# Loads of the second token half's operands: issued by GpSimd instead of SyncE, in a kernel that sums a gated long convolution and a feed-forward layer

## The chip, the cores and the metric

The kernel runs on one core of a Trainium2 chip. The metric is the device time of one execution in microseconds (us), as the median of several runs. A separate execution was recorded by the hardware profiler; every view quoted below is of that one execution. The engines are PE (TensorE: matmuls; its weight loads are shown as PEld), DVE (VectorE), ACT (ScalarE), POOL (GpSimd) and SP (SyncE, which here only issues DMAs). A name with a q behind it (SPq, ACTq) is an engine's sequencer. L477 is line 477 of the kernel.

## The reference

With S = 2048 tokens, D = 576 channels and 4608 hidden units:

```python
xn = layernorm(q)
k_shift = causal_conv(k, shift_k)              # 4 taps per channel
kv = k_shift * v
y = long_causal_conv(kv, ssm_k) + kv * ssm_D   # 2048 taps per channel, by FFT
out = q + xn * y + relu(xn @ w1) @ w2          # w1: 576x4608, w2: 4608x576
```

All in float32. (q is the kernel's x.)

## The kernel before

**The feed-forward layer.** The 2048 tokens are 16 tiles of 128, in two halves of 8. A half is two blocks of 512 tokens. The hidden units are taken 256 at a time, in 18 groups for each half, so there are 36 groups of work, numbered g from 0 to 35; from g = 3 on such a group is a "quad". g = 17 (`NQ - 1`) is the last group of the first half, and g = 18 the first of the second. The first 512 of the 576 channels go through a scheme with seven products for eight (Strassen's kind). It needs seven combinations of the transposed, normalized tokens, the *operands*: "00", "01", "11", "s1", "s2", "s3", "s4", each 128 partitions x 2 x 2 x 512 numbers of 4 bytes (1 MB). The last 64 channels are done the plain way by `rest`, with one *rest operand* `hl` for each block (256 KB). Each number is split into a high and a low part, so that a product is three matmuls (high x high, high x low, low x high). Operand and weights both have the two parts.

**One quad, in PE's order.** First product "00" with weights `wa`; then "01" with `wa`, and the rest of block 0 with `wr`; "s2" with `wb`; "s1" with `wc`; "s3" with `wb`; the rest of block 0 with `wr`; "s4" with `wd`; the rest of block 1; "11" with `wc`; the rest of block 1. Between them stand eight units of the second layer (`mm2`, matmuls into `pso`) that belong to the group before. In the trace the operands are named x and xs (the digits are left out), the products' accumulators psh, and the first layer's low parts ll.

**The weights.** `load_w1(g)` fetches a group's first-layer weights into the tile r1 (0.66 MB in three DMAs, L494 and L497), `load_w2` a piece of the second layer's (288 KB, L505); after g = 0 both are issued by GpSimd. In the profile these tiles are all called r. `load_w1(g + 2)` stands near the end of quad g in the program, once the splits that read the tile before are issued: r1 has one buffer. `split_w` (L512, L513) makes the two parts: ACT writes the high one and GpSimd subtracts for the low one. `sums` (L525) adds weights on DVE for `wb` and `wc`.

**The convolution** is a stream of small steps (`conv`), taken between the products by `tick`, so that PE has their matmuls (L762, into psf and psg) among its own. It is done as a two-stage Fourier transform, with loads of k and v from SP (L164) and stores to DRAM in between (zx, zk, zy).

**The second half's operands** are made early, within the stream (`later_operands`): normalized, transposed, combined, split, and stored in DRAM (`ops_n`, `hl_n`). An operand has one buffer on the chip. So in quad 17, as soon as the product that reads an operand of the first half for the last time is traced, `later` calls `load_operand` (L477) or `load_rest_operand` (L480) for its successor. Such a load waits for that product. Quad 18 and all that follow read the new ones. There are nine of these loads: seven of 1 MB and two of 256 KB, 7.9 MB (1.05 million bytes each for the seven).

**Order.** Instructions of one engine are issued in order, so an instruction that waits holds up what stands behind it on that engine. The order is set when the kernel is built, by a scheduler that runs a model of time (`schedule_with_timeline_sim=True`): among what the model takes to be ready, it puts the earlier in the program first. `issue_after` adds an order by hand. PE's order is fixed in this way from end to end; that of GpSimd and SP is left to the scheduler, within the data's dependences. DMAs issued by SP go out on queue q1, those of GpSimd on q0, those of ACT on q10.

Of the kernel before, what the change touches and what calls it, by code (L numbers as in the profile page):

```python
# [10 lines left out]
F32 = mybir.dt.float32  # L11
# [21 lines left out]
HB = NB // HALVES  # L33
# [66 lines left out]
def h3_ffn_kernel(ctx: ExitStack, tc, x, k, v, shift_k, ssm_k, ssm_D, w1, w2, fwd, inv, mid, out):  # L100
    nc = tc.nc
# [27 lines left out]
    ops_n = {o: dram.tile([P, 2, 2, 512], F32, name=f"ops_{o}") for o in OPERANDS}  # L129
    hl_n = dram.tile([HB, P, 512], F32, name="hl_n")  # L130
# [67 lines left out]
    def operand(o, tag=None):  # L198
        xo[o] = xp.tile([P, 2, 2, 512], F32R, tag=f"x{tag or o}", name=f"x{o}")
        return xo[o]  # L200

    def rest_operand(b):
        hl[b] = xp.tile([P, 512], F32R, tag=f"hl{b % HB}", name=f"hl{b}")
        return hl[b]
# [269 lines left out]
                yield W_FS  # L474

    def load_operand(o):
        nc.sync.dma_start(operand(o).bitcast(F32), ops_n[o])  # L477

    def load_rest_operand(b):
        nc.sync.dma_start(rest_operand(b).bitcast(F32), hl_n[b - HB])  # L480

    def at_turn(g):

# [144 lines left out]
    def quad(g, units):  # L628
# [8 lines left out]
        def later(o):  # L637
            if g == NQ - 1:
                (load_operand if isinstance(o, str) else load_rest_operand)(o)
# [664 lines left out]
```

## Time and profile before

| | |
|---|---|
| median of 3 runs | 1030.0 us (1029.59 to 1030.02) |
| the profiled execution's own time | 1038.15 us |
| its span, first to last instruction | 1036.3 us |
| mean granted TensorE clock | 0.996 |
| DMA bytes moved | 184.69 MB, mean 178 GB/s |
| the nine operand loads, issued by SP | from 447.8 to 478.7 us of the span |
| quad 17, by its first product and that of quad 18 | 446.3 to 478.5 us |

The times in the views count from the start of the span. In the first part of the page each engine has its busy time, its share of the span and its number of instructions. A row of a timeline is start, duration, engine, line, operation, output<-inputs, shapes and count, with the engine's idle time before it and what ended it in brackets. A row of the DMA view is output<-input, issuing queue, count, KB each, and the median time from issue to landing.

### The profile page before, as it was taken

What the parts mean: (1) busy time and instruction counts of PE and PEld (TensorE: products, weight loads), DVE (VectorE), ACT (ScalarE), POOL (GpSimd) and SP (SyncE); (2) the same over time, 40 slices, a digit from 0 to 9 for tenths busy, and PEclk for the clock granted to TensorE, in tenths of its full rate; (3) what the DMA queues carried; (4) which work ended last, traced back from release to release, by engine and by line L of the source; (5) the groups of instructions that cost most, each with busy time, mean ns of one, the idle gap of its engine ahead of it and who ended that gap; (6) DMA issues with size and microseconds to landing.
All of it is one profiled execution on the core that took longest, in us unless ns stands there. A gap on an engine that the chain in (4) does not pass through costs nothing.

```text
span 1036.3 us, 17434 instructions
## 1 busy us (share of the span) xinstructions
PE 1019.9 (98%) x6506; PEld 846.6 (82%) x6506; DVE 702.4 (68%) x1075; ACT 431.4 (42%) x770; POOL 463.6 (45%) x502
## 2 busy tenths in 40 slices
PE   8999999999999999989999999999999999999997
PEld 5898999998988888878878888866777777788777
DVE  6787677775565556778787889455666666556764
ACT  7244334443354444434444444544444445332120
POOL 3335444555443555544555455314424245244450
PEclk9999999999999999998999999999999999999999
DMA  7114364479445473379944433677877887757684
GB/s 175 52 49 118 114 162 126 154 216 199 115 127 172 160 245 104 126 216 322 277 139 132 129 103 115 210 221 227 242 212 226 250 256 226 221 177 230 208 259 114
DMA packets 130848, 184.69 MB, mean 178 GB/s; under 512 B 69213, under 2 KB 81631, under 8 KB 129868
## 3 DMA queue, kind: packets, MB, share of 16 engines
q1 hardware_dynamic: 76180, 123.48, 39.9%
q0 software_dynamic: 16048, 52.44, 16.9%
q10 hardware_dynamic: 38536, 7.66, 3.9%
q8 instruction: 51, 0.84, 0.3%
q14 instruction: 33, 0.27, 0.1%
HBM read 119.04 MB, written 45.61 MB: 159 GB/s over the span
## 4 chain that ended last, share of the span: by engine, by line
PE 88%; DMA 4%; DVE 3%; ACT 2%; issue 1%; POOL 1%; ACTq 1%; SPq 0%; DVEq 0%; POOLq 0%
PE pso L569 40%; PE psh L569 34%; PE psf L762 6%; PE psg L762 4%; PE psh_c L569 3%; DMA r<-in_w 2%; DMA zk<-area 1%; DMA acc<-in_x 1%; ACTq L809 0%; DVE area L1047 0%; DVE area L941 0%; DVE area L942 0%; ACT x L291 0%; DMA area<-in_k 0%; DVE sums L525 0%
## 5 line engine op out<-in xcount | busy, mean ns | idle before, releaser
L569 PE MATMUL pso<-w,hh 128*128 128x288 f32 x2304 | 467.9, 296 | 0.0
L569 PEld LDWEIGHTS pso<-w,hh 128*128 128x128 f32 x2304 | 378.1, 188 | 35.9 <-issue 14.8
L569 PE MATMUL pso<-w,ll 128*128 128x288 f32 x1152 | 339.5, 295 | 0.0
L749 DVE TENSOR_TENSOR acc<-pso,acc 128x576 f32<-128x576 f32 x243 | 183.1, 754 | 167.3 <-PE pso L569 166.9
L569 PEld LDWEIGHTS pso<-w,ll 128*128 128x128 f32 x1152 | 216.4, 188 | 0.0
L513 POOL TENSOR_TENSOR wb<-sums,wb 128x512 fp32r<-128x512 f32 x33 | 52.4, 1587 | 251.1 <-ACT wb L512 217.9
L513 POOL TENSOR_TENSOR w<-r,w 128x576 fp32r<-128x576 f32 x72 | 108.2, 1510 | 118.6 <-ACT w L512 118.6
L569 PE MATMUL psh<-xs,wb 128*128 128x512 f32 x396 | 102.7, 394 | 0.0
L569 PE MATMUL psh<-x,wa 128*128 128x512 f32 x396 | 102.5, 394 | 0.1
L569 PE MATMUL psh<-hl,wr 128*128 128x512 f32 x264 | 85.7, 406 | 3.6 <-ACT psh L686 3.1
L569 PEld LDWEIGHTS psh<-x,wa 128*128 128x128 f32 x396 | 72.4, 188 | 15.3 <-ACT psh L648 0.5
L569 PEld LDWEIGHTS psh<-xs,wb 128*128 128x128 f32 x396 | 70.6, 188 | 14.6 <-issue 3.2
L513 POOL TENSOR_TENSOR wa<-r,wa 128x512 fp32r<-128x512 f32 x36 | 56.1, 1558 | 57.2 <-ACT wa L512 57.1
L762 PE MATMUL psf<-area 64*64 64x512 f32 (+10 forms) x664 | 75.2, 489 | 1.6 <-DVE area L1047 1.0
L593 DVE SCALAR_TENSOR_TENSOR ll<-psh,hh 128x512 fp32r<-128x512 f32 x66 | 45.2, 685 | 37.6 <-ACT hh L591 37.2
L686 ACT ACTIVATE psh<-psh 128x512 f32<-128x512 f32 x33 | 19.2, 582 | 116.5 <-DVE u L684 114.6
L569 PEld LDWEIGHTS psh<-hl,wr 128*128 128x128 f32 x264 | 46.3, 189 | 23.0 <-issue 10.5
L591 ACT ACTIVATE hh<-psh 128x512 fp32r<-128x512 f32 x66 | 39.3, 596 | 50.8 <-PE psh L569 50.1
L1020 ACT ACTIVATE area<-psg 128x1024 f32<-128x1024 f32 x34 | 33.0, 1024 | 53.7 <-PE psg L762 53.7
L591 ACT ACTIVATE hh<-p 128x512 fp32r<-128x512 f32 x33 | 20.9, 632 | 81.9 <-PE pso L569 46.9
L569 PE MATMUL psh<-xs,wd 128*128 128x512 f32 x198 | 52.6, 401 | 0.0
L1047 DVE TENSOR_TENSOR area<-psf,area 128x512 f32<-128x512 f32 x72 | 44.7, 682 | 11.6 <-DMA area<-area 8.4
(134 smaller groups left out, 1487.0 us busy)
## 6 DMA issues: line engine op xcount, KB each, us to landing
r<-in_w POOLq DMA_DIRECT2D x70, 288.0 KB, 3.8
area<-area SPq DMA_DIRECT2D x144, 128.0 KB, 4.0
r<-in_w POOLq DMA_DIRECT2D x35, 512.0 KB, 4.8
zk<-area SPq DMA_DIRECT2D x64, 144.0 KB, 2.2
area<-zk SPq DMA_DIRECT2D x18, 512.0 KB, 4.5
area<-zx SPq DMA_DIRECT2D x18, 512.0 KB, 4.1
zy<-area SPq DMA_DIRECT2D x36, 256.0 KB, 4.7
area<-zy SPq DMA_DIRECT2D x32, 288.0 KB, 4.3
```

Of the source, the lines that this page charges most:

```text
L513: nc.gpsimd.tensor_tensor(w[:, 1, :n], src, w[:, 0, :n], OP.subtract)
L569: last = nc.tensor.matmul(ps, a, m, start=start and n == 0, stop=n == len(seq) - 1, skip_group_check=True)
L591: done["act"] = nc.scalar.activation(hh, ps, AF.Relu)
L593: nc.vector.scalar_tensor_tensor(ll, ps, 0.0, hh, op0=OP.max, op1=OP.subtract)
L686: nc.scalar.activation(x, y, AF.Copy, scale=-1.0)
L749: done["acc"] = nc.vector.tensor_tensor(two(acc[t]), ps[:, :, :NH], two(acc[t]), OP.add)
L762: done["pe"] = nc.tensor.matmul(ps, a, m, start=start, stop=stop, skip_group_check=True)
L1020: nc.scalar.activation(dst, src, AF.Copy)
L1047: nc.vector.tensor_tensor(filt[:, c, k, :], banks[k], filt[:, c, k, :], OP.mult)
```

## The change

The two functions that load the second half's operands issue their DMA from GpSimd. Source, destination, size and the places of the calls stay the same.

```diff
     def load_operand(o):
-        nc.sync.dma_start(operand(o).bitcast(F32), ops_n[o])
+        nc.gpsimd.dma_start(operand(o).bitcast(F32), ops_n[o])
 
     def load_rest_operand(b):
-        nc.sync.dma_start(rest_operand(b).bitcast(F32), hl_n[b - HB])
+        nc.gpsimd.dma_start(rest_operand(b).bitcast(F32), hl_n[b - HB])
```

They are called in quad 17 alone, after each product that reads the old operand for the last time:

```python
def later(o):
    if g == NQ - 1:
        (load_operand if isinstance(o, str) else load_rest_operand)(o)
```

## The prediction

> **What bounds the kernel now.** I read the page first, then the waits of PE, then the chain of waits and the busy time by stage around the nine loads that move. The page:
>
> ```profile
> span 1036.3 us, 17434 instructions
> PE 1019.9 (98%) x6506; PEld 846.6 (82%) x6506; DVE 702.4 (68%) x1075; ACT 431.4 (42%) x770; POOL 463.6 (45%) x502
> PEclk9999999999999999998999999999999999999999
> ```
>
> PE is busy for 98% of the span, so a change that adds no PE work can only touch the 16.4 us in which PE is idle, and the slices in which its clock is low. There is one such slice, the nineteenth (466 to 492 us). The waits of PE over the whole span (engine and line, what it waited for, total, times, longest):
>
> ```profile
> PE psh L569 <- ACT psh L686: 3.1, 2, 2.6
> PE psg L762 <- ACT acc L742: 2.9, 1, 2.9
> ```
>
> The single wait of 2.9 us lies where the operands are reloaded. The busy time in stretches of 5 us there (PE, PEld, DVE, ACT, POOL, then granted clock, DMA share, GB/s):
>
> ```profile
> 450.00:455.00 5.00, 5.00 (x32) 4.52 (x31) 4.93 (x7) 2.39 (x4) 4.99 (x6) 1.00 0.68 229
> 455.00:460.00 5.00, 5.00 (x33) 4.62 (x32) 2.22 (x4) 1.82 (x3) 1.47 (x2) 1.00 1.02 328
> 460.00:465.00 5.00, 2.78 (x25) 1.57 (x23) 1.06 (x3) 1.07 (x3) 0.35 (x1) 0.99 1.04 286
> 465.00:470.00 5.00, 4.36 (x22) 2.76 (x23) 4.67 (x5) 3.16 (x6) 4.61 (x5) 0.50 1.01 405
> 470.00:475.00 5.00, 5.00 (x30) 4.67 (x29) 2.27 (x4) 1.12 (x2) 0.00 (x0) 0.83 1.01 367
> 475.00:480.00 5.00, 5.00 (x29) 4.36 (x28) 5.00 (x7) 2.88 (x6) 1.86 (x2) 1.00 0.77 264
> ```
>
> PE stops for 2.9 us, and then its granted clock is 0.50 and 0.83. The low clock costs 4.36 x 0.50 = 2.2 us and 5.00 x 0.17 = 0.85 us. With the 2.86 us of the stop, **this stall is worth 5.9 us**. The DMA engines are full from 455 to 475. The chain of waits says why PE stopped (start, us, what):
>
> ```profile
> 452.37 11.48 DMA r<-in_w
> 463.93 0.07 ACT wa L512
> 464.47 0.58 ACT p L669
> 465.05 0.55 ACT acc L742
> 465.64 1.99 PE psg L762 x16
> ```
>
> r is the first-layer weight tile of quad 18. GpSimd issued its three loads from 452.37, and they landed at 463.85. ACT's split of r (L512) stood first in ACT's order, and the copy that PE needed stood behind it. From landing to PE is 465.64 - 463.85 = 1.8 us, and PE was ready at 465.64 - 2.86 = 462.8: **r must land by 461.0** for no stall. What r usually takes, and what its loads cost GpSimd, from the view of tile r:
>
> ```profile
> DMA to landing us min/median/max: 2.9/4.3/11.5
> L494 POOL DMA_DIRECT2D r<-in_w x35: 756/773/952, 16.6 to 960.4; - x35
> L505 POOL DMA_DIRECT2D r<-in_w x70: 537/559/563, 23.7 to 972.1; - x70
> ```
>
> So this landing is the longest of all. What the DMA engines did while r was under way, from the DMA view of 452.4 to 463.9:
>
> ```profile
> DMA packets 786, 3.00 MB, mean 261 GB/s; under 512 B 139, under 2 KB 139, under 8 KB 603
> q1 hardware_dynamic: 503, 2.05, 65.0%
> q0 software_dynamic: 282, 0.93, 27.2%
> xs<-ops_s SPq DMA_DIRECT2D x3, 1024.0 KB, 12.8
> x<-ops SPq DMA_DIRECT2D x1, 1024.0 KB, 11.2
> area<-in_k SPq DMA_DIRECT2D x2, 144.0 KB
> ```
>
> q0 is GpSimd's queue, with r (0.66 MB) and a second-layer weight; q1 is SP's, with the operands. 3.00 MB moved before r had landed, though r and the loads issued with it or just before (operand 01 of 1.05 MB, and k and v, 0.59 MB) make only 2.3 MB. So bytes of operands issued after r, from 457.26 on, went out ahead of the last bytes of r: **the two queues share the engines, and r loses by it**.
>
> **The change part by part.** Nine issues leave SP, and nine come to GpSimd. Bytes, tiles and what each load waits for stay. The two queues around the first loads, SP's and then GpSimd's:
>
> ```profile
> 447.83 4.93 SPq L477 DMA_DIRECT2D x<-ops  x2
> 457.26 4.84 SPq L477 DMA_DIRECT2D xs<-ops_s  x3
> ```
> ```profile
> 446.93 1.75 POOL L513 TENSOR_TENSOR wb<-sums,wb 128x512 fp32r<-128x512 f32 x1 [7.14 <-ACT wb L512]
> 449.85 1.30 POOL L513 TENSOR_TENSOR wr<-r,wr 128x256 fp32r<-128x256 f32 x1
> 451.13 1.29 POOL L513 TENSOR_TENSOR wc<-sums,wc 128x512 fp32r<-128x512 f32 x1
> 452.37 0.78 POOL L494 DMA_DIRECT2D r<-in_w  x1
> 478.14 1.83 POOL L513 TENSOR_TENSOR wb<-sums,wb 128x512 fp32r<-128x512 f32 x1 [8.53 <-ACT wb L512]
> 483.51 0.77 POOL L494 DMA_DIRECT2D r<-in_w  x1
> ```
>
> *GpSimd's time.* No load of 1 MB from GpSimd is in the trace. The rows give 0.56 us for 288 KB and 0.77 us for 512 KB; scaled by bytes, 1 MB would be 1.55 us. I take 0.56 to 0.77, since r's 0.77 us belongs to a load in four pieces per partition and an operand is one piece: nine issues, 5 to 7 us (at most 12). GpSimd is idle for over half of the stage, 8.53 us in one piece ahead of 478.14, so I cost this at nothing. The place without cover is the issue of operand 00: if it stands among the splits, wr ends later than 451.15, and PE reads wr next:
>
> ```profile
> 452.22 0.62 PE L569 MATMUL psh<-hl,wr 128*128 128x512 f32 x2
> ```
>
> The slack is 1.07 us. An issue of 0.56 to 0.77 us fits; 1.55 us would cost 0.5 us.
>
> *The added waits.* Each load waits on its new engine for the last product that reads the old operand. Operand 00's is over about 447.8, while GpSimd works on wb, so it waits for nothing. Operand 01's ends about 452.4, when r is issued anyway. For s2, s1 and s3 GpSimd waits at most from 456.8 to about 461.8. Behind it stands the split of wa of quad 18, which PE needs only from 478. Nothing to pay.
>
> *What the move frees.* On one queue, operands issued after r no longer pass it. With operand 00's issue ahead and 01's behind, r goes out at about 453.0. Ahead of it or beside it are r itself, k and v, 1.25 MB, at 261 GB/s 4.8 us: r lands at about 458, 3 us before the limit. If 01's load is issued first, 1.05 MB more, it lands at about 462 and PE stops for 0.8 us, less than the other stop of the trace (2.6 us). The stall goes in both orders: **-5.9 us**, or -5.1. SP's own loads of k and v come out from behind the operands' waits. They wait for DVE later and bound nothing: 0.
>
> *What is late next.* Quad 18 starts 5.9 us earlier, but the bytes do not go faster. Its own weight load, r of quad 19, is issued at 483.51, and on ACT it reads:
>
> ```profile
> 491.58 0.64 ACT L512 ACTIVATE wa<-r 128x512 fp32r<-128x512 f32 x1 [1.10 <-DMA r<-in_w]
> 492.12 0.58 ACT L669 ACTIVATE p<-psh 128x512 f32<-128x512 f32 x1
> 493.92 0.63 PE L569 MATMUL psh<-hl,wr 128*128 128x512 f32 x2
> ```
>
> It lands late already, but PE needs the copy of 492.12 only at 493.92: slack 493.92 - 492.70 = 1.2 us. The idle DMA time that can be filled is 0.32 x 5 us in 450 to 455 and 0.23 x 5 us in 475 to 480, 2.75 us. So r of quad 19 comes 5.9 - 2.75 - 1.2 = 1.9 us too late for PE: **+1.9 us**. The ends are 0 (operand 11, in front of r on one queue, is done by then) and 4.7 us (no idle time can be used).
>
> *Sum:* -5.9 + 1.9 = **-4.0 us** on the profiled execution, whose own time is 1038.15 us. The median of the runs shown is 1030.0 us, 8 us less: the stall may be smaller where nothing is recorded, which the rivals take up. Forecast: 1030.0 - 4.0 = **1026.0 us**, its own range 1022 to 1028.
>
> **The rivals.** *The engines are shared whoever issues* (chance 0.17): the bytes are the same, the DMA share is 1.0 from 455 to 475, and r lands as late as before because it waits for bytes and not for a queue. Time 1030. The Trainium skill has this as a rule (DMA: Bandwidth & Descriptors, "Issuing engines are not separate DMA queues"): DMAs from any issuer run on the same 16 engines and interleave, and a second issuer saves only issue time. By that rule the sum would be 0. Against it stand the 3.00 MB ahead of the end of r; the same page ("Queues, rings and completion order") has each engine take turns between queue rows, which fits them.
>
> *The stall belongs to the profiled execution* (0.10): 1038.15 - 1030.0 = 8.15 us is more than the 5.9 us. Then there is nothing to win: 1030.
>
> *r queues behind the operands* (0.18), the slower side. On one queue r cannot pass what is in front of it, and the operands' landings are 11.2 and 12.8 us long in the DMA view. If GpSimd issues 01 before r, r ends behind it at 452.4 + 11.2 + 2.9 = 466.5, 2.6 us later than now. Quad 19's r, behind operand 11 (issued after the splits, about 482), ends at 482 + 11.2 + 2.9 = 496.1, 4.6 us after the 491.5 of now, of which 1.2 us is slack: +3.4 us. Together +6.0: 1036, and up to 1039 if a second low-clock stretch follows. It decides by r's landing: after 463.9, this rival is right. Against it: r's loads stand before 01's in the program, and by 452.4 both can be issued.
>
> *More than the forecast* (0.05): the 2.6 us wait for L686 goes as well, because SP's loads are earlier. 1030.0 - 5.9 - 2.6 = 1021.5.
>
> **How the numbers follow.** The forecast has 0.50, then 0.17, 0.10, 0.18 and 0.05. About 0.2% (2.1 us) is what a measurement of this kernel can tell from no change. Faster: forecast and the last, less a little for a forecast that ends within 2.1 us: 0.53. Same: 0.17 + 0.10 and that little: 0.28. Slower: 0.19, with the bound of late wr. The range takes in the forecast, both rivals at 1030 and the lower part of the slower one: 1021.5 to 1034.
>
> **What would show it.** Right: r of quad 18 lands by 461, PE's wait for L742 is gone, no low slice in PEclk; a wait for r in quad 18 of 1 to 4 us. The first step is wrong if r still takes over 10 us; the cover is wrong if PE waits for GpSimd's wr or wb. If the profile loses its stall and the times stay, the stall belonged to the profile. The prediction fails most easily by the order that the scheduler gives GpSimd's queue, which the trace of before cannot show.

## The result, and the profile after

The change makes the kernel slower. Before: 1029.8 us (1029.03 to 1030.02, 4 runs); after: 1036.01 us (1034.62 to 1036.74, 4 runs); ratio 1.006, 95% interval 1.0043 to 1.0078. In a later session it was 1035.44 us (1033.41 to 1038.55, 6 runs) against 1029.98 us (29 runs), ratio 1.0051 (1.0031 to 1.0071). So the loss is 5.5 to 6.2 us, where a gain of 4 was forecast; 1036.0 lies above the range's end of 1034.0.

The page of the changed kernel:

```profile
span 1035.0 us, 17432 instructions
PE 1019.7 (99%) x6506; PEld 846.9 (82%) x6506; DVE 705.4 (68%) x1075; ACT 431.8 (42%) x770; POOL 463.7 (45%) x511
PEclk9999999999999999999999999999999999999999
```

and the head of its PE waits over the whole span:

```profile
PE psh L569 <- ACT psh L648: 2.5, 1, 2.5
PE psf L762 <- issue: 1.4, 1, 1.4
PE psf L762 <- DVE area L1047: 1.4, 4, 0.9
```

The wait for L742 that stood in the profile of before is gone; two new ones stand in its place. The busy time in stretches of 5 us (PE, PEld, DVE, ACT, POOL, clock, DMA share, GB/s):

```profile
460.00:465.00 5.00, 5.00 (x47) 3.35 (x46) 4.42 (x5) 3.23 (x5) 4.98 (x6) 1.00 1.00 335
465.00:470.00 5.00, 5.00 (x37) 4.83 (x36) 3.29 (x5) 1.12 (x2) 1.65 (x4) 1.00 1.03 422
470.00:475.00 5.00, 5.00 (x29) 4.40 (x28) 5.00 (x6) 2.88 (x6) 2.52 (x4) 1.00 1.03 412
475.00:480.00 5.00, 2.46 (x18) 2.22 (x17) 5.00 (x5) 0.58 (x1) 4.60 (x6) 1.00 1.01 413
480.00:485.00 5.00, 5.00 (x21) 4.35 (x21) 3.87 (x6) 1.82 (x3) 0.65 (x1) 0.66 1.05 295
```

From 460 to 475, where before stopped and ran at 0.50 and 0.83, PE is full at a clock of 1.00. The stop now comes at 475 to 480, just behind the turn from quad 17 to 18 (472.5), and the low clock, 0.66, behind it. GpSimd's row at the start of the stage and ACT's split of r of quad 18, from the timeline:

```profile
448.47 1.25 POOL L513 TENSOR_TENSOR wd<-r,wd 128x256 fp32r<-128x256 f32 x1
449.67 0.55 POOL L477 DMA_DIRECT2D x<-ops  x1
450.25 0.75 POOL L513 TENSOR_TENSOR wr<-r,wr 128x256 fp32r<-128x256 f32 x1
...
452.20 0.79 POOL L494 DMA_DIRECT2D r<-in_w  x1
...
454.02 0.57 POOL L477 DMA_DIRECT2D x<-ops  x1
```
```profile
458.65 0.64 ACT L512 ACTIVATE wa<-r 128x512 fp32r<-128x512 f32 x1 [0.66 <-DMA r<-in_w]
```

The order is the one that was assumed: operand 00 among the splits, then r, then operand 01. r was there at 458.65 (forecast: about 458, against 463.85 in the one profile of before). So this part of the forecast came out. Why is the kernel slower?

### The profile page after: what moved, and what is told of

Read it like the earlier page. It is cut to its first block, busy times and chain, and to the rows that moved or that the text cites. A ratio compares the mean times of both kernels' runs of the same rounds, so it can differ in the third digit from the quotient of the medians.

```text
span 1035.0 us, 17432 instructions
## 1 busy us (share of the span) xinstructions
PE 1019.7 (99%) x6506; PEld 846.9 (82%) x6506; DVE 705.4 (68%) x1075; ACT 431.8 (42%) x770; POOL 463.7 (45%) x511
## 4 chain that ended last, share of the span: by engine, by line
PE 91%; DVE 3%; ACT 2%; DMA 1%; issue 1%; ACTq 0%; POOL 0%; SPq 0%; DVEq 0%; POOLq 0%
PE pso L569 42%; PE psh L569 35%; PE psf L762 6%; PE psg L762 4%; PE psh_c L569 3%; PE psw L1211 1%; DMA area<-area 1%; DVE area L1047 1%; DMA r<-in_w 1%; ACTq L809 0%; DVE ll L593 0%; DVE area L946 0%; DVE area L941 0%; ACT x L291 0%; DVE sums L525 0%
## 5 line engine op out<-in xcount | busy, mean ns | idle before, releaser
L762 PE MATMUL psf<-area 64*64 64x512 f32 (+10 forms) x664 | 75.4, 489 | 3.5 <-issue 1.4
L513 POOL TENSOR_TENSOR wa<-r,wa 128x512 fp32r<-128x512 f32 x36 | 53.5, 1487 | 46.5 <-ACT wa L512 46.5
L593 DVE SCALAR_TENSOR_TENSOR ll<-psh,hh 128x512 fp32r<-128x512 f32 x66 | 45.2, 685 | 38.3 <-ACT hh L591 38.2
L686 ACT ACTIVATE psh<-psh 128x512 f32<-128x512 f32 x33 | 19.2, 582 | 112.5 <-DVE u L684 110.5
L1020 ACT ACTIVATE area<-psg 128x1024 f32<-128x1024 f32 x34 | 33.0, 1024 | 55.6 <-PE psg L762 55.6
L1047 DVE TENSOR_TENSOR area<-psf,area 128x512 f32<-128x512 f32 x72 | 44.7, 682 | 15.4 <-DMA area<-area 6.5
L569 PE MATMUL psh<-x,wc 128*128 128x512 f32 x198 | 51.7, 396 | 0.0
```

The source lines that it names most:

```text
L513: nc.gpsimd.tensor_tensor(w[:, 1, :n], src, w[:, 0, :n], OP.subtract)
L569: last = nc.tensor.matmul(ps, a, m, start=start and n == 0, stop=n == len(seq) - 1, skip_group_check=True)
L593: nc.vector.scalar_tensor_tensor(ll, ps, 0.0, hh, op0=OP.max, op1=OP.subtract)
L686: nc.scalar.activation(x, y, AF.Copy, scale=-1.0)
L762: done["pe"] = nc.tensor.matmul(ps, a, m, start=start, stop=stop, skip_group_check=True)
L1020: nc.scalar.activation(dst, src, AF.Copy)
```

## The experiments

Sixteen runs, in four groups; the runs of before beside them had medians of 1029.9, 1029.8, 1030.3 and 1030.0 us. No edit changes the output. A kernel's PE order is the same in all of them (the names of the matmuls agree one by one, but for four of 6506 in one profile), so the start of the k-th matmul of a kernel less that of before, in its second profile, tells where time is lost.

### Is the stall of the profiled execution there at all?

The kernel before, profiled again.

> The kernel of before unchanged, to see an ordinary execution of it. Theory A (the profiled execution of before, 1038.15 us, was an unusual one: its two stops of PE, 2.9 us with 3.0 us of low clock behind it in quad 17 and 2.6 us in quad 19, are absent when the kernel takes 1030): span about 1028, no wait of PE for L742, granted clock 1.0 from 465 to 475, r of quad 18 landing under 10 us. Rival C (the stops are in every execution, and recording adds the rest): the stop of 2.9 us and the low clock are there again, whatever the time.

1029.2 us. The windows where the first profile had its stall and the changed kernel its stop, and ACT's split of r of quad 18:

```profile
460.00:465.00 5.00, 5.00 (x48) 3.39 (x47) 4.78 (x6) 4.24 (x7) 4.07 (x4) 1.00 1.04 348
465.00:470.00 5.00, 5.00 (x36) 4.79 (x35) 3.96 (x7) 1.12 (x2) 0.92 (x2) 1.00 1.01 413
470.00:475.00 5.00, 5.00 (x30) 4.40 (x29) 5.00 (x7) 2.89 (x6) 2.67 (x2) 1.00 1.07 402
475.00:480.00 5.00, 5.00 (x34) 4.59 (x33) 4.96 (x7) 1.45 (x3) 4.53 (x6) 1.00 1.01 304
```
```profile
460.21 0.63 ACT L512 ACTIVATE wa<-r 128x512 fp32r<-128x512 f32 x1 [2.01 <-DMA r<-in_w]
```

There is no wait for L742 and no low clock, and r was there at 460.21, ahead of the limit of 461.0, with the operands on SyncE. The other stop of the first profile (2.6 us, for L686) is missing too. Of 85 timed runs of before, the highest took 1034.86 us; the profiled one took 1038.15. The 5.9 us were **a stop that comes in some executions**: of the eleven other profiles in which SyncE issues the early operands, one has it, with 3.2 us (the kernel with operand 11 and rest 3 on GpSimd, below). In the six profiles where GpSimd issues the early operands it is not seen; but none in six against two in twelve can be chance, so it is not shown that the move prevents it.

What the move does for r is smaller than the first profile made it look. ACT's split of r began 6.4 to 6.8 us after r's issue in those six profiles, 7.1 to 8.1 us in the ten ordinary ones with SyncE, and 11.6 and 11.9 us in the two with the stop. So about 1 us of the 5 comes from the move, and the median holds nothing of it.

### Which of the nine loads costs?

Operand 11 and the rest operand of block 3, the last two of the nine, go back to SyncE; and the reverse, those two alone on GpSimd.

```diff
-        nc.gpsimd.dma_start(operand(o).bitcast(F32), ops_n[o])
+        (nc.sync if o == "11" else nc.gpsimd).dma_start(operand(o).bitcast(F32), ops_n[o])
...
-        nc.gpsimd.dma_start(rest_operand(b).bitcast(F32), hl_n[b - HB])
+        (nc.sync if b == 3 else nc.gpsimd).dma_start(rest_operand(b).bitcast(F32), hl_n[b - HB])
```

> The changed kernel, but operand 11 and the rest operand of block 3 are loaded by SyncE as before; the seven earlier loads stay on GpSimd. Theory A (the loss is at the turn from quad 17 to 18: the issues of these two loads stand ahead of and among GpSimd's splits wb, wd, wr, wc, DVE's L946 takes 3.33 us and L593 2.44 us beside them, PE waits 2.5 us and has a low clock after): 1030 to 1031.5, both DVE instructions under 2 us, no wait of PE for L648 over 1 us. Rival B (the loss comes from 7 MB of operands on GpSimd's queue, which delays the convolution's transfers or the weights): 1034 to 1036, about as the changed kernel.

> The other part alone: only operand 11 and the rest operand of block 3 go through GpSimd, the seven earlier loads through SyncE. Theory A: 1033.5 to 1036, with the stretched DVE instructions and the wait of PE at the turn of quad 17 to 18. Rival B: 1030 to 1031, since five sixths of the bytes are back on SyncE's queue.

Seven on GpSimd and the last two on SyncE: 1030.75 us (10 runs), ratio 1.0007 (0.9997 to 1.0016), and no matmul's start differs from before by more than 0.3 us from there on (0.03 us at the end). Only the last two on GpSimd: 1033.71 us (9 runs), ratio 1.0031 (1.002 to 1.0041). So seven loads of the nine cost nothing, and two cost about 4 us. In the second kernel's profile both stops are seen, the chance one and the one of the change (PE's waits, 440 to 500):

```profile
PE psg L762 <- ACT acc L742: 3.2, 1, 3.2
PE psh L569 <- ACT psh L648: 2.6, 1, 2.6
```

### What the last two do at the turn

The timeline of the changed kernel from 472 (start, us; DVE's operations beside GpSimd's):

```profile
472.46 0.53 POOL L477 DMA_DIRECT2D x<-ops  x1 [4.60 <-PE psh L569]
...
472.70 3.33 DVE L946 TENSOR_TENSOR area<-area 128x576 f32<-128x576 f32 x1
473.01 1.30 POOL L513 TENSOR_TENSOR wb<-sums,wb 128x512 fp32r<-128x512 f32 x1
...
474.27 0.73 POOL L513 TENSOR_TENSOR wd<-r,wd 128x256 fp32r<-128x256 f32 x1
474.95 0.57 POOL L480 DMA_DIRECT2D hl<-hl_n  x1
475.54 1.08 POOL L513 TENSOR_TENSOR wr<-r,wr 128x256 fp32r<-128x256 f32 x1
475.95 2.44 DVE L593 SCALAR_TENSOR_TENSOR ll<-p,hh 128x512 fp32r<-128x512 f32 x1
...
476.59 1.26 POOL L513 TENSOR_TENSOR wc<-sums,wc 128x512 fp32r<-128x512 f32 x1
...
479.09 0.58 ACT L648 ACTIVATE psh<-psh 128x512 f32<-128x512 f32 x1 [5.31 <-DVE ll L593]
```

and of before (the second profile):

```profile
472.33 1.83 POOL L513 TENSOR_TENSOR wb<-sums,wb 128x512 fp32r<-128x512 f32 x1 [6.40 <-ACT wb L512]
...
472.91 1.85 DVE L946 TENSOR_TENSOR area<-area 128x576 f32<-128x576 f32 x1
...
474.11 1.25 POOL L513 TENSOR_TENSOR wd<-r,wd 128x256 fp32r<-128x256 f32 x1
...
474.69 1.22 DVE L593 SCALAR_TENSOR_TENSOR ll<-p,hh 128x512 fp32r<-128x512 f32 x1
...
476.60 0.58 ACT L648 ACTIVATE psh<-psh 128x512 f32<-128x512 f32 x1 [2.61 <-DVE ll L593]
```

In before GpSimd and DVE take turns: each operation waits for one of the other engine's (wd takes 1.25 us for the 0.73 it needs, L946 1.85 for 0.75). In the changed kernel the load of operand 11 waits for the product that reads the old one, until 472.46, and so stands directly ahead of the split of wb. Then wb and wd run one after the other at full speed and DVE's L946 waits for both; L593 waits for wr and wc. L648, which PE needs, comes at 479.09 and not at 476.60, 2.5 us late, and PE stops for 2.5 us.

The Trainium skill (SBUF — State Buffer, "Who interferes with whom") states that a DVE instruction with two inputs in SBUF contends with a GpSimd instruction that reads SBUF, and calls the port pair that they share an exclusive lock. The trace agrees in kind: L946 and the L593 on p and hh are held up, while in before the L593 on psh (in PSUM) takes its 0.68 us beside wr. The section does not say that DVE's waiting operation is passed by several of GpSimd's in a row, which these rows show.

Four kernels take the two issues apart. First, the two loads are left where they are on GpSimd but carry 8 bytes of each partition; SyncE loads the rest (in the line below, `some` is true for these two loads). Then each load alone:

```diff
+    def parts(to, src, some): [q.dma_start(to[:, s], src[:, s]) for q, s in (((nc.gpsimd, slice(0, 2)), (nc.sync, slice(2, None))) if some else ((nc.sync, slice(0, None)),))]
```
```diff
+        (nc.gpsimd if o == "11" else nc.sync).dma_start(operand(o).bitcast(F32), ops_n[o])
```
```diff
+        (nc.gpsimd if b == 3 else nc.sync).dma_start(rest_operand(b).bitcast(F32), hl_n[b - HB])
```

> The kernel before, but of operand 11 and of rest operand 3 GpSimd loads the first 8 bytes of each partition, at the places where the changed kernel issues them (ahead of wb, and between wd and wr), and SyncE all the rest. The bytes are as before on SyncE's queue; what comes to GpSimd is two issues and their waits. If the issues among GpSimd's splits make the loss at the turn (they hold the splits up or bring them beside DVE's operations): the additions of DVE in 472 to 479 take over 2 us as in the changed kernel, PE stops for about 2.5 us and the clock falls after it, 3 to 4 us, 1032.5 to 1034. If the bytes on GpSimd's queue make it: DVE's operations take 0.7 us, no stop, 1029 to 1030.5.

> The kernel before, with only operand 11 loaded by GpSimd (ahead of the split of wb of quad 18; 1 MB). If this issue alone brings GpSimd's splits beside DVE's additions at the turn: DVE over 2 us for one of them, a stop of PE of 2 to 3 us, 1032 to 1034 as with both. If the issue of rest operand 3, between wd and wr, does it: no loss here, 1029 to 1030.5. If it takes both, half of it or less: 1030.5 to 1031.5.

> The kernel before, with only the rest operand of block 3 loaded by GpSimd, between the splits of wd and wr of quad 18. In the trace of before the four splits there alternate with DVE's operations (L946 1.85 us, L593 1.22). If an issue directly ahead of a row of splits lets GpSimd's splits pass DVE one after another: the alternation holds until the issue, then the operation of DVE that comes up during it waits for wr and wc and takes over 2 us; the copy for PE (L648) is late by 0 to 1.5 us and the loss at the turn is 0 to 1.5 us; 1030 to 1031.5. If the issue alone costs (0.55 us of GpSimd, no passing): no operation of DVE over 2 us, no loss; 1029 to 1030.5.

With slivers of 8 bytes: 1033.92 us (5 runs), ratio 1.0038 (1.0026 to 1.0051), L946 3.34 us, L593 2.44, PE's wait for L648 2.5. So **it is the issue, not the bytes**. Operand 11 alone: 1034.90 us (5 runs), ratio 1.0041 (1.0027 to 1.0056); in its profile 2.4 us are lost at the turn, and 3.3 at a stop at 520 such as the first profile of before has too (2.3 us), so its time is not the price of the issue alone. Rest operand 3 alone: 1029.85 us (11 runs), ratio 0.9998 (0.9988 to 1.0009), no operation of DVE at the turn over 1.9 us. So it is the issue ahead of wb; the one between wd and wr costs nothing, and the half of its expectation that saw DVE passed there was wrong. With operand 11 alone, nothing stands between the four splits, and the timeline shows the plain case:

```profile
472.55 0.53 POOL L477 DMA_DIRECT2D x<-ops  x1 [7.20 <-PE psh L569]
...
472.79 4.87 DVE L946 TENSOR_TENSOR area<-area 128x576 f32<-128x576 f32 x1
473.10 1.30 POOL L513 TENSOR_TENSOR wb<-sums,wb 128x512 fp32r<-128x512 f32 x1
...
475.75 1.28 POOL L513 TENSOR_TENSOR wc<-sums,wc 128x512 fp32r<-128x512 f32 x1
```

L946 began before wb and ended at 477.66, 0.6 us after wc. In the changed kernel DVE got through at the issue of rest 3, between wd and wr, but PE's stop is no shorter for it (2.5 us, against 2.3 with operand 11 alone). The trace of before shows the same once, where it costs PE nothing, at the end of quad 21:

```profile
585.31 0.54 POOL L815 DMA_DIRECT2D area<-in_fwd  x1 [6.24 <-PE psf L762]
585.51 3.65 DVE L942 TENSOR_TENSOR area<-area 128x576 f32<-128x576 f32 x1
...
585.86 1.29 POOL L513 TENSOR_TENSOR wb<-sums,wb 128x512 fp32r<-128x512 f32 x1
```

The fourth kernel keeps all nine on GpSimd but issues the last two behind the splits:

```diff
+    def late_loads():
+        with tc.issue_after(done["pool"].ins): load_operand("11"), load_rest_operand(3)
...
-            if g == NQ - 1:
+            if g == NQ - 1 and o not in ("11", 3):
...
-        split_c(g)
+        split_c(g); g == NQ and late_loads()
```

> All nine loads stay on GpSimd; operand 11 and the rest operand of block 3 are issued behind the split of wc of quad 18, and not ahead of wb and between wd and wr. Theory A: 1030 to 1031.5, since GpSimd's splits start as early as before, with nothing between them; it tells the place of the two issues from the engine that makes them. Rival B: 1034 to 1036.

1034.06 us (6 runs), ratio 1.0042 (1.0027 to 1.0057). The time is the one that was expected of the rival, and the trace shows why it does not speak for it. The turn is free: DVE and GpSimd alternate as in before, and PE does not stop. But 1.1 us are lost at 493 (r of quad 19 is issued behind operand 11 and comes late), and 2.0 us at 677 to 684. ACT's row of the first:

```profile
490.81 0.63 ACT L512 ACTIVATE wa<-r 128x512 fp32r<-128x512 f32 x1 [1.72 <-DMA r<-in_w]
```

### The second loss, 200 us later

The changed kernel also loses 2.1 us at 677 to 684 (before's time; 1.7 us in its second profile), in quad 25, long after the loads. The load concerned is that of r of quad 26; the expectations name it by the quad in which it is issued, 25, and the next one likewise. The chain in the second profile of the changed kernel (1033.88 us):

```profile
665.09 0.77 POOL L494 DMA_DIRECT2D r<-in_w  x1 [1.12 <-issue]
...
669.34 0.63 ACT L512 ACTIVATE wa<-r 128x512 fp32r<-128x512 f32 x1 [0.55 <-DMA r<-in_w]
669.88 2.04 ACT L1020 ACTIVATE area<-psf 128x512 f32<-128x512 f32 x4
...
671.45 2.52 SPq L1025 DMA_DIRECT2D area<-area  x4
...
678.88 2.49 DVE L1047 TENSOR_TENSOR area<-psf,area 128x512 f32<-128x512 f32 x4 [5.29 <-DMA area<-area]
680.27 1.07 PE L762 MATMUL psf<-area 64*64 64x512 f32 x4 [1.03 <-issue]
```

The issue of r begins 1.12 us after GpSimd is done with the split before it, and no row says what it waits for. r is late, ACT's split of it stands in front of the copies L1020, the copies' stores L1025 go out late, and PE waits for what DVE makes of them. Less the 2.0 us by which this kernel is late already, the split begins 0.6 us later than in before and L1047 1.7 us later; how the one grows to the other is not shown. In the three kernels run until then that have this wait (the changed one, the last two loads alone on GpSimd, and those two behind the splits; in the second it stands one load of r later, at 705), the DMAs that GpSimd had issued until then come to **28,416 rows** (a row is one piece of a transfer, as the trace's record of the issue counts them: 512 + 64 + 64 for the three loads of r, 128 for a second-layer load, 128 for an operand). The theory: GpSimd waits when its count of rows passes a fixed place, and nine loads more, 1152 rows, bring that place from a harmless issue to the one of r. Nine small DMAs in quad 20 add the rows without the operands, and nine of 16 rows the number without the rows:

```diff
+    nc.gpsimd.memset(sign, 1.0); pad = const.tile([P, 18], F32, name="pad")
...
+    def extra():
+        with tc.issue_after(done["pool"].ins): [nc.gpsimd.dma_start(pad[:128, 2 * i:2 * i + 2], w1[:128, 2 * i:2 * i + 2]) for i in range(9)]
...
-        split_w2(g, 1)
+        split_w2(g, 1); g == 20 and extra()
```

> The kernel before, with all nine operand loads on SyncE, and nine more DMAs from GpSimd in quad 20, each 128 rows of 8 bytes into a tile that nobody reads. So GpSimd has issued as many DMAs and as many rows as in the changed kernel by quad 23, while neither operands nor traffic move. Theory D (GpSimd stops before an issue when its count of DMA rows reaches a fixed place, 28,416 rows in the three kernels that show it): the L494 of r of quad 25 waits 1.1 us at about 662, r lands later, and PE loses 1.4 to 2 us at 670 to 680, none at the turn from quad 17 to 18; time 1031 to 1032. Theory L (the count of DMAs and not of rows shifts which semaphores they use): the same. Theory O (the late r belongs to the operands' loads themselves): no wait there, 1029 to 1030.

> As the kernel with nine extra DMAs of 128 rows, with 16 rows each: nine DMAs more, but 144 rows in place of 1152. Theory D: the place of 28,416 rows is reached about 1,000 rows later than there, at the issue of another load, so the L494 of r of quad 25 waits for nothing and PE loses nothing at 670 to 680; 1029 to 1030. Theory L: the wait of 1.1 us stays at the same L494, and the time is that of the kernel with 128 rows.

> The kernel with nine extra DMAs of 128 rows once more, for a second profile: its profiled execution was the fastest of five (1032.4, median 1035.1). If the rest of the loss lies at the late r of quad 25 too: PE loses 3 to 6 us at 670 to 690, against 2.6 us in the first profile. If the nine issues cost by themselves: a loss in quads 20 and 21, at 560 to 590.

> The kernel with nine extra DMAs of 16 rows once more, for a second profile: its median was 2.7 us above before, and the first profile shows no loss at quads 20 to 26. If the nine issues cost by themselves: a loss at 560 to 590 here. If the shifted place costs, now at the L494 of r of quad 26: a loss at 700 to 725. If neither: 1029 to 1031, and chance.

128 rows: the wait of 1.12 us at that load is there, at 28,416 rows, and PE loses 2.4 us at 677 in the first profile and 3.2 in the second. 16 rows: no wait there and 0.3 us lost at 677; the wait has moved one quad on, to a place where r has time:

```profile
697.92 0.77 POOL L494 DMA_DIRECT2D r<-in_w  x1 [1.23 <-issue]
```

There 28,304 rows had been issued, and this load's 512 end at 28,816. So the theory of the count of DMAs alone falls. But rows alone do not give one place either: in the kernels with one of the last two loads on GpSimd the same load ends at 28,800 rows and does not wait, nor do the 64 rows behind it, to 28,864; the next 64 do (operand 11 alone):

```profile
702.84 0.53 POOL L497 DMA_DIRECT2D r<-in_w  x1 [0.73 <-issue]
```

Both counts enter. Beside the rows, the trace has 16 packets of 4 bytes for each DMA of GpSimd. Counted with these, the issues that wait here all end at 31,664 (28,816 + 16 x 178) or more, and the last ones ahead of them at 31,600 (28,864 + 16 x 171) or less. Nine DMAs of 128 rows move it by 1296, nine of 16 rows by 288. But the times were too high for it: 1035.13 us (5 runs, ratio 1.0043, 1.0029 to 1.0057) and 1032.55 us (11 runs, ratio 1.0024, 1.0014 to 1.0033), then 1038.39 and 1033.87 us in the second profiles, with losses at 245, 269, 392 and 520, ahead of the extra DMAs. So neither a cost of the nine issues nor the later r explains them, and part of each expectation failed.

The place was also shifted in the changed kernel, by four such DMAs (512 rows), first with their target on the chip:

> The changed kernel, with four more DMAs of 128 rows of 8 bytes from GpSimd in quad 20, into a tile that nobody reads: work is added. Theory D (GpSimd waits 1.1 us at the issue whose rows go past 28,800 to 28,816): the 512 rows bring that place from the L494 of r of quad 25 to a second-layer load (L505) at about 653, behind which GpSimd is idle; r of quad 25 is on time, the loss of 2.0 us at 677 to 684 is gone, the one at the turn stays: 1033 to 1034.5, faster than the changed kernel's 1036.0. If the late r has another cause, or the extra issues cost by themselves: 1036 to 1038.

1036.98 us (6 runs), ratio 1.0068 (1.0053 to 1.0083): not faster, though the wait at that load was gone and the loss at 677 was 1.2 us and no longer 2.1. ACT's split of r and the stores L1025 were on time there (within 0.1 us), so these 1.2 us have another cause, which is not known. It also had a stop at 392, so the tile itself came under suspicion. It was tried alone, and both edits with a target in DRAM:

```diff
+    nc.gpsimd.memset(sign, 1.0); pad = const.tile([P, 18], F32, name="pad"); nc.gpsimd.memset(pad, 0.0)
```
```diff
+        with tc.issue_after(done["pool"].ins): [nc.gpsimd.dma_start(pad[:, 2 * i:2 * i + 2], w1[:P, 2 * i:2 * i + 2]) for pad in [dram.tile([P, 18], F32, name="pad")] for i in range(9)]
```

> The kernel before with nothing but the tile of the extra DMAs, 72 bytes of each partition, set to zero at the start: no extra DMA. All kernels with this tile lost 1 to 4 us at 245, 392 and 520, ahead of the extra DMAs or far behind them. If the tile (it moves the addresses of what is allocated behind it) makes that: 1031.5 to 1033, as the kernel with nine DMAs of 16 rows. If the nine DMAs make it: 1029 to 1030.5.

> The kernel before with the nine extra DMAs of 128 rows of 8 bytes in quad 20, now from DRAM to DRAM, so no tile is added on the chip. Theory D (GpSimd waits at the place of 28,800 rows): the L494 of r of quad 25 waits 1.1 us, 2 to 2.6 us are lost at 677, nothing at 245, 392, 520; 1031.5 to 1033. If the nine issues cost by themselves, 1 us or more on top of that in quads 20 and 21.

> The changed kernel with four extra DMAs of 128 rows in quad 20 from DRAM to DRAM. Theory D: the wait leaves the L494 of r of quad 25, the 2.0 us at 677 go, the turn keeps its 3.7 to 4.4 us: 1 to 2 us faster than the changed kernel in the same call. If the place has no part in the loss: as the changed kernel or slower.

> The changed kernel again, beside the others on one chip, for a second profile. By the first: 3.7 to 4.1 us lost at the turn (L648 late behind DVE's L946 of 3.3 us and L593 of 2.4 us), 2.0 us at 677 (r of quad 25 late), 1 to 1.5 us by chance elsewhere; 1034.5 to 1036.7. If one of the two losses is missing here, it was chance in the first profile.

The tile alone, with no DMA: 1031.88 us (12 runs), ratio 1.0015 (0.9999 to 1.0032), with a stop at 392 that costs 4.0 us in its profile. Nine DMAs of 128 rows to DRAM, added to before: 1032.01 us (12 runs), ratio 1.0016 (1.0003 to 1.0029); the wait of 1.12 us at 28,416 rows, and 2.0 us lost at 677. Four of them added to the changed kernel: 1033.76 us (12 runs), against 1035.44 for the changed kernel beside it (6 runs). With more work the median is **1.7 us lower**; but the intervals of the two ratios to before overlap (1.0027 to 1.0055, 1.0031 to 1.0071), so the times alone do not settle it. Its timeline, to be held against the six rows above (take 1.5 us from its times, by which it is later there, chiefly for a stop at 520):

```profile
665.38 0.77 POOL L494 DMA_DIRECT2D r<-in_w  x1
...
670.16 0.63 ACT L512 ACTIVATE wa<-r 128x512 fp32r<-128x512 f32 x1
...
678.86 2.48 DVE L1047 TENSOR_TENSOR area<-psf,area 128x512 f32<-128x512 f32 x4 [3.81 <-DMA area<-area]
680.63 1.94 PE L762 MATMUL psf<-area 64*64 64x512 f32 x8
```

No wait ahead of L494, none of ACT for r, 1.5 us less in front of L1047, and the eight matmuls of L762 in one piece; 0.2 us are lost at 677. The six profiles with the wait at this load lose 1.7 to 3.2 us there, the twelve without it 1.2 us at most. So the second loss is shown in the traces both ways, added and taken away. What is left of this kernel's 3.5 us against before is the turn (2.6 us) and a stop of 1.3 us at 520.

The sum of the parts: the turn costs 2.4 to 2.7 us where the clock stays at 1.00 behind the stop (the changed kernel's second profile, operand 11 alone) and 4.0 to 4.3 where it falls to 0.66 or 0.67 (the first profile, the slivers); the shifted wait costs 1.7 to 2.1 us. Together 4.1 to 6.4 us, against 5.5 to 6.2 measured. Up to 1.5 us more in the profiles is lost at 900 and 995, where kernels with all operands on SyncE lose too (0.8 us at 900 in the one with 16 rows).

**Open.** What decides whether DVE's waiting operation is passed (issue ahead of the row) or let through (all other rows at the turn) was not settled; no kernel delayed wb without a DMA issue. What the wait at a count of rows is for, the trace does not show. Whether the tile of 72 bytes makes the stops at 392 more frequent is not settled either: its interval touches 1.0. And no kernel of these beats before.

## Why the prediction was wrong, point by point

- *r of quad 18 lands by 461, the wait for L742 and the low slice go:* so it came out (458.65, and none of the six profiles with the early operands on GpSimd has that wait), but before's second profile has it too, with r at 460.21. The queue was worth about 1 us of r's landing, not 5, and nothing of the time.
- **The failed step: "Forecast: 1030.0 - 4.0".** The 5.9 us were read from an execution of 1038.15 us and taken off a median of 1030.0 that does not hold them. Before's second profile has no such stop, so there was nothing to win. The rival that named this had the warning number, 8.15 us, and got 0.10. On the gain it was the right one.
- *Nine issues at nothing:* the second failed step. Seven cost nothing (1030.75 us). Operand 11 was put "after the splits, about 482"; it was issued at 472.46, ahead of them, as soon as the product let it go. The cover named, 8.53 us of idle time, ended just there. Its own time, 0.53 us, was sized well (0.56 to 0.77); the price is that DVE's operations behind it are passed by GpSimd's splits: L648 2.5 us late, 2.4 to 4.3 us in all. The sign was in the trace of before, at 585 us, and was not read.
- *Added waits at nothing:* right for wa of quad 18 and for s2, s1, s3. wr's slack held: the issue of operand 00 stood ahead of wr and PE did not wait.
- *+1.9 us for r of quad 19:* not paid in the changed kernel, where PE comes to it late behind its stop; 1.1 us where the turn is free and r is issued behind operand 11. The sum left out that a stop at the turn would cover it.
- *Missing:* the shifted wait at r of quad 26, 1.7 to 2.1 us. Nothing in the profile of before would have shown where it falls.
- *The rivals:* "r queues behind the operands" names 1036, the time that came, by luck: r of quad 18 was not behind operand 01, and its term for quad 19 shows in one kernel alone. "Engines are shared" is right that the move wins no time; r did come about 1 us earlier with the same bytes and a DMA share of 1.0, so the queue counts for a little. The wait for L686 of "More than the forecast" is missing in the changed kernel, and in before's second profile as well.

## What to carry to other kernels

A profile that is 0.8% longer than the median holds a stop that the median lacks: take a gain from it only if a second profile shows the stop too. Moving DMA issues to an engine that also computes puts each of them at a place in that engine's row, so look at where the load's wait ends and what stands right behind it, not at the engine's idle share. An issue of 0.53 us there cost up to 4 us, through an engine that appears in neither the diff nor its dependences.

## What the runs showed of the hardware that was not expected

- Behind a DMA issue of GpSimd, two to four of its subtractions in a row ran at full speed (1.30, 0.73, 0.73, 1.28 us) while an addition of DVE with both inputs on the chip took 3.3 to 4.9 us for its 0.75.
- GpSimd waited 1.1 to 1.2 us before a load of r in ten profiles, and 0.7 us between two small loads in two, with the issue that took its rows plus 16 for each DMA past a place between 31,601 and 31,664. In the other six a second-layer load passes that place, and none of them shows such a wait. In every profile there is one of 1.8 us at a load that takes the rows from 14,848 to 15,360. With 512 idle rows ahead of it the wait left r of quad 26, and the changed kernel's loss there fell from 1.7 to 0.2 us.
- In ten profiles with SyncE issuing the operands, r's split began 7.1 to 8.1 us after r's issue; in the six with the early operands on GpSimd's queue, 6.4 to 6.8 us.
- Issuing 1 MB from GpSimd took 0.53 to 0.58 us, no more than 256 KB (0.54 to 0.57).
